# Two units' maxima transposed side by side in one PSUM bank, and stand-in products in place of a memset of the P @ V bank

## The chip, the cores and the metric

The kernel runs on one NeuronCore of a Trainium2 chip. The metric is the device time of one execution in microseconds (us). The profile is that of one execution, taken by the hardware profiler. The engines are TensorE (PE; its weight loads are listed as PEld), VectorE (DVE), ScalarE (ACT), GpSimd (POOL) and SyncE (SP), which here only issues transfers.

## The reference, cut to what matters

Two attentions over the same x (2048 tokens, 512 channels, 32 heads of 16) are mixed by a gate. Side A is plain attention over all 2048 keys. Side B is attention within segments of 512 tokens, masked, plus a memory term that is linear in the queries.

```python
p = softmax(q_A @ k_A.T * 0.25);  a = (p @ v_A) @ wo_A
for s in range(4):                       # segments of 512 tokens
    p = softmax(q_B[s] @ k_B[s].T * 0.25 + mask)
    o[s] = g * (phi(q_B[s]) @ M) / (phi(q_B[s]) @ z + 1e-6) + (1 - g) * (p @ v_B[s])
    M, z = M + phi(k_B[s]).T @ v_B[s], z + sum(phi(k_B[s]))
out = gate * a + (1 - gate) * (o @ wo_B)
```

A softmax subtracts the maximum of each row of scores ahead of its exponential. The change is about how that maximum gets to where it is subtracted.

## The kernel before, in words

**Two stages.** Up to about 326 us the kernel projects x to q, k and v for both sides, stores them to HBM, and begins with the maxima. Then comes the long loop over score slots, and from about 1810 us the last output products.

**Units and slots.** A unit is a side, a group of four heads and a chunk of 512 queries; there are 32 of side A and 32 of side B, mostly taken in turn A, B, A, B (line 99). An A unit has 64 slots and a B unit 10 (`SLOTS`), together 2368, so that a pair of units takes 74 slots. In a slot (`score_part`, line 641) PE multiplies keys by queries into one of three `st` banks (line 656) and ACT takes the exponential into SBUF (line 679). The products use half of PE's rows each: four heads stand as h = 0, 1 in rows 0 to 49 and h = 2, 3 in rows 64 to 113, and slots take the heads in the order 0, 2, 1, 3.

**Maxima, 96 slots ahead.** In the same slot PE makes a second product, of queries by keys, for a unit that is 96 slots (`LEAD`) further on (`max_part`, line 207; products at line 204), into one of four `sm` banks, and DVE reduces it to row maxima (lines 219, 240, 244). For the masked blocks of side B, ACT copies the bank to SBUF (line 230), POOL masks the copy, and DVE reduces it eight slots later (line 234).

**From maxima to scores.** When a unit's last maximum is made, `finish_max` (line 176) has DVE reduce the partial maxima (line 180 or 182) and POOL split the negated result into a rounded part and its remainder, `ms` (lines 187, 188). The unit goes on the list `late` with a due slot: the slot m of its last maximum + 18 (line 248). `transpose_max` (line 191) then takes an `st` bank, transposes `ms` with an identity product (line 194, 32 columns of weights, 128 columns streamed, fp32, which the profile shows as two passes), has ACT copy the bank's 32 rows to `mt` (line 196), and has SP issue two transfers from `mt` into rows 48, 49 and 112, 113 of the unit's q tile (line 198). The k tiles hold ones in those rows, so that the product of a score has the maximum subtracted already. A unit's first score waits for the first of its two transfers (rows 48, 49: heads 0 and 1), its second score, of head 2, for the other.

**Bursts.** After every third slot (`BURST`) comes what is not a score: products P @ V of probabilities that are at least three (A) or five (B) slots old, three pieces a time or four when the queue is long (`some_values`, line 691; line 712), or pieces of the output product (line 789, four strips of 32 columns); then the transposes that are due (line 887). P @ V gathers all pieces of a unit in one bank, `ops` (line 608); each of the four heads has a strip of 32 rows, of which 17 are written, and ACT copies the whole bank out when a unit is done (line 716). For that the bank is set to zero once, by DVE (line 609). After the bursts of slots 2 and 5, when there is no P @ V yet, PE makes three products of the identity by itself into the bank's first 128 columns (line 885).

**Order.** The order of all engines is written out: each engine works through its instructions in the order of these calls. SP's list holds, beside the transfers of the maxima, loads of k (lines 158, 159), q (146, 147) and v (623, 626), and the stores.

Of the kernel before, what the change touches and what calls it, by code (L numbers as in the profile page):

```python
# [10 lines left out]
F32 = mybir.dt.float32  # L11
F32R = mybir.dt.float32r
# [28 lines left out]
MASK_T = 8  # L41
LATE_T = 8
# [5 lines left out]
def gated_mix(ctx, tc, x, xT, wqkv, a_wo, b_wq, b_wk, b_wv, b_wo, beta, gate_w, out):  # L48
    nc = tc.nc
# [24 lines left out]
    identf = const.tile([128, 128], F32, name="identf")  # L74
# [18 lines left out]
    mp = ctx.enter_context(tc.tile_pool(name="mp", bufs=2))  # L93
# [18 lines left out]
    for k in range(NU):  # L112
        mine = {u: iter(range(32)) for u in range(2)}
        bs = [k - 1] if 0 < k < NU - 1 else [k - 1, k] if k else []
        start, apart = (34, 3) if k == 1 else (6, 7) if k < NU - 1 else (24, 3)
        theirs = {r: [(unit("B", b), (r, i)) for b in bs for i in range(5)] for r in range(2)}
        for p in range(64 + 10 * len(bs)):
            r = (len(maxs) + 1) % 2
            i = (p - start) // apart
# [8 lines left out]
    qt, kt_ = {}, {}  # L128

    def raw(t):  # L130

        return t[:].bitcast(F32)
# [36 lines left out]
    late = []  # L169
# [6 lines left out]
    def finish_max(u):  # L176
        nm = mp.tile([128, 4, 4], F32, tag="nm", name="nm")
        pm = pmt.pop(u)
        if u[0] == "A":
            nc.vector.tensor_reduce(nm, pm, axis=AX.X, op=ALU.max, negate=True)  # L180
        else:
            nc.vector.tensor_reduce(nm.rearrange("p h (a b) -> p (h a) b", b=2),
                                    pm.rearrange("p b h (a k) -> p (h a) b k", a=2), axis=AX.X, op=ALU.max, negate=True)

        ms = mp.tile([128, 2, 2, 2, 4], F32R, tag="ms", name="ms")
        nv = nm.rearrange("p (r h) s -> p r h s", r=2)
        nc.gpsimd.tensor_copy(ms[:, :, 0], nv)  # L187
        nc.gpsimd.tensor_sub(ms[:, :, 1], nv, ms[:, :, 0].bitcast(F32))
        return ms

    def transpose_max(u, ms, pool, tag):

        pt = pool.tile([128, CH], F32, tag=tag, name="mt_ps")
        nc.tensor.matmul(pt[:32, :128], ms.rearrange("p r a h s -> p (r a h s)").bitcast(F32), identf, start=True, stop=True)  # L194
        mt = mp.tile([32, 128], F32R, tag="mt", name="mt")
        nc.scalar.copy(mt, pt[:32, :128])  # L196
        for r in range(2):
            nc.sync.dma_start(raw(qt[u])[64 * r + 48:64 * r + 50], raw(mt)[16 * r:16 * r + 16])

    def blocked(ps):  # L200
        return ps.rearrange("p (b t) -> p b t", t=128)

    def max_product(ps, u, h, s, n0, n, k, k0=0):
        nc.tensor.matmul(ps[:, n0:n0 + n], rows(qt[u][:, :, s * 128:(s + 1) * 128], h, 48), rows(k[:, :, k0:k0 + n], h, 48),  # L204
                         start=True, stop=True)

    def max_part(m, bank):

        u, (r, i) = maxs[m]
        side, g, c = u  # L210
        if u not in pmt:
            pmt[u] = mp.tile([128, 4, 4, 4], F32, tag="pmA", name="pm") if side == "A" else pmB[(c * NG + g) % 2]
        pm = pmt[u]
        ps = bank()
        if side == "A":

            kc, s, h = i // 8, i % 8 // 2, 2 * r + i % 2
            max_product(ps, u, h, s, 0, CH, kt_[u, kc])
            nc.vector.tensor_reduce(pm[:, h, s, kc:kc + 1], ps, axis=AX.X, op=ALU.max)  # L219
        else:  # L220


            k = kt_[u, c]
            h0 = 2 * r
            if i < 2:
                for n in range(4):
                    b = i + 2 * (n % 2)
                    max_product(ps, u, h0 + n // 2, b, 128 * n, 128, k, 128 * b)
                dg = dp.tile([128, 4, 128], F32, tag="dg", name="dg")
                nc.scalar.copy(dg, blocked(ps))  # L230
                nc.gpsimd.affine_select(out=dg, in_=dg, pattern=[[0, 4], [-1, 128]], base=0, channel_multiplier=1,  # L231
                                        compare_op=ALU.is_ge, fill=MASKED)
                to = pm[:, i, h0:h0 + 2, 3::4] if i == 0 else pm[:, i, h0:h0 + 2, 1::6]
                todo.append((m + MASK_T, lambda: nc.vector.tensor_reduce(  # L234
                    to, dg.rearrange("p (h s) t -> p h s t", h=2), axis=AX.X, op=ALU.max)))
            elif i < 4:
                h = h0 + i - 2
                max_product(ps, u, h, 1, 0, 128, k)
                max_product(ps, u, h, 3, 128, 384, k)
                nc.vector.tensor_reduce(pm[:, 1, h, 3:7], blocked(ps), axis=AX.X, op=ALU.max)  # L240
            else:
                for f in range(2):
                    max_product(ps, u, h0 + f, 2, 256 * f, 256, k)
                nc.vector.tensor_reduce(pm[:, 0, h0:h0 + 2, 4:6], ps.rearrange("p (h b t) -> p h b t", h=2, b=2), axis=AX.X,
                                        op=ALU.max)
        if m == last_max[u]:
            def finish():
                late.append((m + MASK_T + 2 + LATE_T, u, finish_max(u)))
            todo.append((m + (MASK_T + 1 if side == "B" else 0), finish))

    def run_todo(m):

        for e in [e for e in todo if e[0] <= m]:
            todo.remove(e)
            e[1]()

    def run_late(pool, tag, m):
        for e in [e for e in late if e[0] < m]:
            late.remove(e)
            transpose_max(e[1], e[2], pool, tag)  # L260

    loaded = [0]

    def loads(m):

        m = min(m, len(maxs) - 1)
        while loaded[0] <= m:
            u, (r, i) = maxs[loaded[0]]
            if loaded[0] == first_max[u]:
                load_q(u)  # L270
            kc = u[2] if u[0] == "B" else i // 8
            if (u, kc) not in kt_:
                load_k(u, kc)
            loaded[0] += 1
# [3 lines left out]
    with ExitStack() as p0:  # L278
# [264 lines left out]
        def some_max():  # L543
            m = mnext[0]
            if m == LEAD:
                return
            loads(m + 3 + PRE)
            for i in range(4):
                max_part(m + i, lambda: me_sm.tile([128, CH], F32, tag="sm", name="sm"))
            run_todo(m + 3)  # L550
            mnext[0] += 4
            run_late(me_ps, "me", mnext[0])
# [53 lines left out]
    banks = [sm_ps.tile([128, CH], F32, name=f"sm{i}") for i in range(4)]  # L606

    ops = o_ps.tile([128, CH], F32, name="ops")
    nc.vector.memset(ops, 0.0)

    wos = {}

# [239 lines left out]
    def jam(n):  # L852


        if n < first["A", 0, 1]:
            return len(queue) > 10
        return (len(queue) > 6) + (len(queue) > 13 and n >= first["A", 0, last])
# [3 lines left out]
    while n < nS or queue or beside or filled[0] < len(fill):  # L861
        for f in beside.pop(n, []):
            f()
        if n < nS:
            score_part(n)
        m = n + LEAD
        if m < nS:
            loads(m + PRE)

            def bank():  # L870
                i = free.pop(0)
                free.append(i)
                return banks[i]
            max_part(m, bank)
        run_todo(m)
        if n % BURST == BURST - 1 or n >= nS:
            if shared:
                for _ in range(4):
                    shared.pop(0)()
            else:  # L880
                some_values(n, MOST + jam(n) if n < nS else 8)
            if n < 6:

                for _ in range(3):
                    nc.tensor.matmul(ops[:, :128], identf, identf, start=True, stop=True)

            if any(e[0] < m + 1 for e in late):
                run_late(st_ps, "st", m + 1)
            else:
                if filled[0] < len(fill) and fill[filled[0]][0] <= n:  # L890
                    fill[filled[0]][1]()
                    filled[0] += 1
        n += 1
# [11 lines left out]
def build():  # L905
    import concourse.bacc as bacc
    nc = bacc.Bacc("TRN2", target_bir_lowering=False, num_devices=1)
    shapes = {"x": (S, D), "xT": (D, S), "wqkv": (D, 3 * D), "a_wo": (D, D), "b_wq": (D, D), "b_wk": (D, D),
              "b_wv": (D, D), "b_wo": (D, D), "beta": (H,), "gate_w": (D,)}
    args = [nc.dram_tensor(n, s, F32, kind="ExternalInput").ap() for n, s in shapes.items()]  # L910
    out = nc.dram_tensor("out", (S, D), F32, kind="ExternalOutput").ap()
    with tile.TileContext(nc) as tc:
        gated_mix(tc, *args, out)
    return nc
# [23 lines left out]
```

## Time and profile before

| | |
|---|---|
| time, median of 3 runs | 1890.31 us (1885.98 to 1891.0) |
| time of the profiled execution | 1884.44 us |
| its span, first to last instruction | 1882.4 us |
| busy: PE, DVE, ACT, POOL | 99%, 85%, 80%, 17% |
| granted clock of TensorE | 1.0 |
| transposes of maxima (line 194) | 64, as 128 passes of 273 ns (median) |
| ACT's copies of them (line 196) | 64, 254 ns (median) |
| transfers of the maxima (line 198) | 128, issued in 617 (A) and 660 ns (B) (medians) |
| memset of the P @ V bank (line 609) | 1, 485 ns |

A row of the trace names a line, an engine, an operation and tiles as "out<-in". [...] Transfers appear as issues on SP (SPq); the time of landing is that of the last update of the transfer's semaphore.

### The profile page before, as it was taken

To read this page: it belongs to the slowest core of one execution; us is meant where nothing else is said; L and a number is where in the kernel's file an instruction comes from. 1 tells how busy PE (TensorE), PEld (TensorE's weight loads), DVE (VectorE), ACT (ScalarE), POOL (GpSimd) and SP (SyncE) were. 2 spreads that over 40 slices of the span, in tenths; PEclk is the share of its full clock that TensorE was granted. 3 is DMA by queue.
4 is the path that set the end of the run, shared out by engine and by line. 5 is a ranking of instruction groups with operands and counts; after the bars stand their busy time and mean duration, and the time that the engine had idled before them with its cause. 6 is when DMAs were issued, how large, how long until landed. Compare 5 with 4: busy or idle time off the path is not lost.

```text
span 1882.4 us, 46526 instructions
## 1 busy us (share of the span) xinstructions
PE 1865.2 (99%) x18149; PEld 1008.7 (54%) x18149; DVE 1596.0 (85%) x2746; ACT 1508.0 (80%) x2929; POOL 314.9 (17%) x515
## 2 busy tenths in 40 slices
PE   9999999999999999999999999999999999999999
PEld 7887676555555554444444444444444455555546
DVE  4235777999999999999999999999999999999820
ACT  5445444898988898888888888888888888888884
POOL 3001222111111111111111111212121211111210
PEclk9999999999999999999999999999999999999999
DMA  7567555234343434343434343434343434333311
GB/s 243 193 227 253 196 183 194 83 112 136 88 109 87 113 91 112 94 115 99 114 95 113 102 113 102 113 98 113 98 111 102 113 103 115 102 103 101 89 55 48
DMA packets 124170, 227.31 MB, mean 121 GB/s; under 512 B 34952, under 2 KB 49960, under 8 KB 123440
## 3 DMA queue, kind: packets, MB, share of 16 engines
q1 hardware_dynamic: 122448, 222.68, 41.1%
q8 instruction: 144, 2.36, 0.6%
q0 software_dynamic: 1216, 1.14, 0.2%
q14 instruction: 74, 0.61, 0.1%
q10 hardware_dynamic: 288, 0.52, 0.1%
HBM read 155.52 MB, written 67.52 MB: 118 GB/s over the span
## 4 chain that ended last, share of the span: by engine, by line
PE 92%; ACT 3%; DMA 2%; DVE 1%; issue 1%; POOL 1%; SPq 0%; ACTq 0%; POOLq 0%; DVEq 0%
PE ops L712 31%; PE st L656 28%; PE sm L204 14%; PE pr L315 10%; PE ops L789 6%; PE sm L789 1%; ACT p L679 1%; POOL mn L375 1%; DMA raw<-xT 1%; PE mt_ps L194 1%; PE num L497 1%; ACT dg L230 0%; DMA qdA<-q 0%; DMA vs<-wqkv 0%; DMA qdB<-q 0%
## 5 line engine op out<-in xcount | busy, mean ns | idle before, releaser
L679 ACT ACTIVATE p<-st 128x512 f32<-128x512 f32 x2304 | 1222.4, 605 | 173.6 <-PE sm L204 141.5
L219 DVE TENSOR_REDUCE pm<-sm 128x1 f32<-128x512 f32 x2048 | 1282.3, 683 | 64.8 <-PE sm L204 48.7
L204 PE MATMUL sm<-kA,qA 48*128 48x512 f32 x2048 | 739.4, 445 | 0.0
L656 PE MATMUL st<-qA,kA 50*128 50x512 f32 x2048 | 693.7, 436 | 3.7 <-ACT p L679 3.2
L656 PEld LDWEIGHTS st<-qA,kA 50*128 50x128 f32 x2048 | 332.8, 185 | 426.6 <-ACT p L679 364.6
L712 PE MATMUL ops<-p,vA 128*17 128x512 f32 (+3 forms) x5848 | 556.4, 469 | 0.0
L204 PEld LDWEIGHTS sm<-kA,qA 48*128 48x128 f32 x2048 | 332.6, 184 | 20.7 <-DVE pm L219 6.7
L712 PEld LDWEIGHTS ops<-p,vA 128*17 128x17 f32 x5848 | 109.7, 95 | 174.2 <-issue 152.7
L204 PE MATMUL sm<-kB,qB 48*128 48x128 f32 (+2 forms) x896 | 168.6, 291 | 0.0
L204 PEld LDWEIGHTS sm<-kB,qB 48*128 48x128 f32 x896 | 134.4, 186 | 8.8 <-DVE pm L219 2.6
L231 POOL TENSOR_SCALAR_AFFINE_SELECT dg<-dg 128x512 f32<-128x512 f32 x128 | 81.2, 635 | 296.0 <-ACT dg L230 296.0
L187 POOL CAST ms<-nm 128x16 fp32r<-128x16 f32 x64 | 12.6, 196 | 644.9 <-DVE nm L180 399.8
L656 PE MATMUL st<-qB,kB 50*128 50x384 f32 (+3 forms) x512 | 119.8, 342 | 0.6 <-ACT mt L196 0.2
L378 DVE TENSOR_TENSOR q<-full,q 128x512 fp32r<-128x512 f32 x64 | 44.1, 689 | 87.1 <-ACT q L371 86.0
L656 PEld LDWEIGHTS st<-qB,kB 50*128 50x128 f32 x512 | 71.5, 185 | 66.3 <-ACT p L679 54.0
L660 POOL TENSOR_SCALAR_AFFINE_SELECT p<-p 128x512 f32<-128x512 f32 x128 | 78.8, 635 | 90.7 <-ACT p L679 88.5
L240 DVE TENSOR_REDUCE pmB<-sm 128x4 f32<-128x512 f32 x128 | 87.3, 682 | 0.5 <-PE sm L204 0.5
L234 DVE TENSOR_REDUCE pmB<-dg 128x4 f32<-128x512 f32 x128 | 86.7, 678 | 0.0
L712 PE MATMUL ops<-p,vB 128*17 128x128 f32 (+3 forms) x1192 | 86.5, 398 | 0.2
L370 ACT COPY full<-pr 128x512 f32<-128x512 f32 x64 | 37.3, 583 | 50.7 <-PE pr L315 50.4
L230 ACT COPY dg<-sm 128x512 f32<-128x512 f32 x128 | 76.4, 597 | 1.0 <-DVE pmB L234 0.6
L789 PE MATMUL ops<-woA,vA 128*32 128x128 f32 x1664 | 66.9, 278 | 3.3 <-ACT oraw L716 3.3
(146 smaller groups left out, 1558.6 us busy)
## 6 DMA issues: line engine op xcount, KB each, us to landing
kA<-kdA SPq DMA_DIRECT2D x256, 128.0 KB
vA<-vdA SPq DMA_DIRECT2D x31, 544.0 KB
kA<-kdA SPq DMA_DIRECT2D x256, 64.0 KB
qdA<-q SPq DMA_DIRECT2D x32, 256.0 KB
kdA<-q SPq DMA_DIRECT2D x32, 256.0 KB
qdB<-q SPq DMA_DIRECT2D x32, 256.0 KB
qA<-qdA SPq DMA_DIRECT2D x64, 128.0 KB
kdB<-q SPq DMA_DIRECT2D x32, 256.0 KB
```

The costliest lines, as they stand in the source:

```text
L204: nc.tensor.matmul(ps[:, n0:n0 + n], rows(qt[u][:, :, s * 128:(s + 1) * 128], h, 48), rows(k[:, :, k0:k0 + n], h, 48), start=True, stop=True)
L219: nc.vector.tensor_reduce(pm[:, h, s, kc:kc + 1], ps, axis=AX.X, op=ALU.max)
L230: nc.scalar.copy(dg, blocked(ps))
L231: nc.gpsimd.affine_select(out=dg, in_=dg, pattern=[[0, 4], [-1, 128]], base=0, channel_multiplier=1, compare_op=ALU.is_ge, fill=MASKED)
L234: todo.append((m + MASK_T, lambda: nc.vector.tensor_reduce(to, dg.rearrange("p (h s) t -> p h s t", h=2), axis=AX.X, op=ALU.max)))
L240: nc.vector.tensor_reduce(pm[:, 1, h, 3:7], blocked(ps), axis=AX.X, op=ALU.max)
L315: nc.tensor.matmul(ps, l(a, k), r(b, k), start=(n == 0), stop=(n == 11))
L656: nc.tensor.matmul(ps[:, n0:n0 + CH - q0], rows(k[:, :, b * 128:(b + 1) * 128], h, 50), rows(q[:, :, q0:], h, 50), start=True, stop=True)
L660: nc.gpsimd.affine_select(out=x, in_=x, pattern=[[0, 4], [1, 128]], base=0, channel_multiplier=-1, compare_op=ALU.is_ge, fill=0.0)
L679: nc.scalar.activation(p[:, h], ps, AF.Exp, scale=SCALE)
L712: nc.tensor.matmul(ops[32 * h:32 * h + 17, q0:q0 + 128 * w], v[:, 17 * h:17 * h + 17], p[:, h, c0:c0 + 128 * w], start=(i == 0), stop=done ...
L789: nc.tensor.matmul(ps[32 * t:32 * t + 32, 128 * (j % (ps.shape[1] // 128)):128 * (j % (ps.shape[1] // 128)) + 128], held[side, c][:, o, 12 ...
```

## The change

Due units are taken from `late` in twos. Both are transposed into one bank: the first into partitions 0 to 31, the second into 32 to 63, by products in the first and the second strip of 32 columns of PE (`tile_position`). One copy by ACT takes both, and SP issues the four transfers, those of the first unit first. An A unit is due four slots earlier than before, 14 slots after its last maximum. The memset of the bank of P @ V is dropped; the products of the identity after slots 2 and 5 are now four each, one for every 128 columns, so that they write the whole bank.

```diff
-    def transpose_max(u, ms, pool, tag):
+    def transpose_max(us, pool, tag):
+        w = 32 * len(us)
         pt = pool.tile([128, CH], F32, tag=tag, name="mt_ps")
-        nc.tensor.matmul(pt[:32, :128], ms.rearrange("p r a h s -> p (r a h s)").bitcast(F32), identf, start=True, stop=True)
-        mt = mp.tile([32, 128], F32R, tag="mt", name="mt")
-        nc.scalar.copy(mt, pt[:32, :128])
-        for r in range(2):
-            nc.sync.dma_start(raw(qt[u])[64 * r + 48:64 * r + 50], raw(mt)[16 * r:16 * r + 16])
+        for i, (_, u, ms) in enumerate(us):
+            nc.tensor.matmul(pt[32 * i:32 * i + 32, :128], ms.rearrange("p r a h s -> p (r a h s)").bitcast(F32), identf,
+                             start=True, stop=True, tile_position=(0, 32 * i))
+        mt = mp.tile([64, 128], F32R, tag="mt", name="mt")
+        nc.scalar.copy(mt[:w], pt[:w, :128])
+        for i, (_, u, ms) in enumerate(us):
+            for r in range(2):
+                nc.sync.dma_start(raw(qt[u])[64 * r + 48:64 * r + 50], raw(mt)[32 * i + 16 * r:32 * i + 16 * r + 16])
...
-                late.append((m + MASK_T + 2 + LATE_T, u, finish_max(u)))
+                late.append((m + MASK_T + 2 + LATE_T - (4 if side == "A" else 0), u, finish_max(u)))
...
     def run_late(pool, tag, m):
-        for e in [e for e in late if e[0] < m]:
-            late.remove(e)
-            transpose_max(e[1], e[2], pool, tag)
+        while us := [e for e in late if e[0] < m][:2]:
+            for e in us:
+                late.remove(e)
+            transpose_max(us, pool, tag)
...
     ops = o_ps.tile([128, CH], F32, name="ops")
-    nc.vector.memset(ops, 0.0)
...
             if n < 6:
-                for _ in range(3):
-                    nc.tensor.matmul(ops[:, :128], identf, identf, start=True, stop=True)
+                for i in range(4):
+                    nc.tensor.matmul(ops[:, 128 * i:128 * i + 128], identf, identf, start=True, stop=True)
```

## The prediction

> **What bounds the kernel now.** I read the stages of the span first, then the groups that touch a transpose, then single bursts on DVE, PE and SP in order of time. In the page, and in the stages cut from the steady loop, the columns are us, busy time and instructions by engine:
>
> ```profile
> PE 1865.2 (99%) x18149; PEld 1008.7 (54%) x18149; DVE 1596.0 (85%) x2746; ACT 1508.0 (80%) x2929; POOL 314.9 (17%) x515
> ```
>
> ```profile
> 400.00:700.00 300.00, 299.58 (x3054) 152.72 (x3042) 292.49 (x501) 267.34 (x529) 45.68 (x86) 1.00 0.36 98
> 700.00:1100.00 400.00, 397.98 (x3965) 186.60 (x3957) 385.68 (x662) 351.90 (x695) 68.19 (x116) 1.00 0.40 105
> 1100.00:1500.00 400.00, 397.30 (x3966) 184.66 (x3964) 386.09 (x663) 351.12 (x691) 68.42 (x115) 1.00 0.41 109
> ```
>
> PE is always "busy", but its matmuls overlap. DVE's reduces do not hide so much: 97% of each stage, 96.4% from 700 us on. Where nothing but scores, maxima and P @ V is in a burst (400 such bursts, 1.88 us each), DVE idles 0.036 us of it: there DVE is the bound and PE waits for its banks. All of DVE's idle time from 411 to 1750 us is 48 us, and it gathers where PE comes late, as after a transpose. So a saving on PE ends the run earlier only as far as DVE was waiting for PE at that place.
>
> **The transposes.** This is the group that the change halves:
>
> ```profile
> L194 PE MATMUL mt_ps<-identf,ms x128: 272/273/297, 309.8 to 1811.8; 128*32 128x128 f32 x128
> L196 ACT CAST mt<-mt_ps x64: 246/254/262, 310.2 to 1812.1; 32x128 fp32r<-32x128 f32 x64
> ```
>
> Which ones pair follows from the due slots. From unit A2 on, a B unit's last maximum comes 4 slots before that of the next A unit. B is due 18 slots after its own, A now 14: the same slot, so both are found after the same burst, and it is B's old burst. That holds for 29 pairs; A0, B0, A1 and the last three stay single. 64 copies become 35, and 29 bursts of an A transpose lose it.
>
> What such a burst costs is seen around a B and an A transpose, PE first, then DVE (start, duration, idle before):
>
> ```profile
> 1075.40 1.05 PE L712 MATMUL ops<-p,vA 128*17 128x512 f32 x8
> 1076.27 0.38 PE L194 MATMUL mt_ps<-identf,ms 128*32 128x128 f32 x2
> 1076.58 0.50 PE L656 MATMUL st<-qA,kA 50*128 50x512 f32 x1
> 1078.41 0.50 PE L656 MATMUL st<-qA,kA 50*128 50x512 f32 x1
> ```
>
> ```profile
> 1075.07 1.89 DVE L219 TENSOR_REDUCE pm<-sm 128x1 f32<-128x512 f32 x3 [0.30 <-PE sm L204]
> 1077.15 1.29 DVE L219 TENSOR_REDUCE pm<-sm 128x1 f32<-128x512 f32 x2 [0.19 <-PE sm L204]
> 1078.98 0.69 DVE L219 TENSOR_REDUCE pm<-sm 128x1 f32<-128x512 f32 x1 [0.55 <-PE sm L204]
> ```
>
> The two passes start 0.109 us apart and the scores follow, so that a transpose holds the stream of PE for 2 x 0.109 = 0.218 us. Does the second of a pair cost it again? The nearest row is the output product, with the same shape (32 columns, 128 streamed, fp32) in four strips:
>
> ```profile
> 1089.38 0.64 PE L789 MATMUL ops<-woA,vA 128*32 128x128 f32 x16
> ```
>
> 16 passes start within 0.46 us (the next 16 at 1089.84); in the single records four strips start 7 ns apart, and the next four passes 0.109 us later. So a pair costs 0.218 + 0.007 us, and 29 x 0.218 = 6.3 us of PE go. If strips did not overlap, nothing would go.
>
> How much of it ends the run? For each of the 29 A transposes I took DVE's idle time in the 2 us behind it. It depends on how many slots lie between the pair's burst and B's first score: with 7, 0.17 us up to 600 us of the span and 0.36 later; with 8, 0.33 and 0.20; with 9, next to none. Summing the smaller of 0.218 and the idle time gives 2.0 + 1.8 + 0.2 = **4.0 us**. The bounds are 0 (DVE finds another wait) and 6.3 (what PE gains beyond is kept as a lead). I take 4.0: in plain bursts DVE leaves no room for a lead. ACT's 29 copies (29 x 0.254 = 7.4 us) I cost at nothing: DVE's idle time was ended by PE's products, and ACT idles 0.26 us in a plain burst. Were they not hidden, it would be a gain: rival 1.
>
> **A rule on the array.** The first pass of a transpose starts 0.109 us after the last pass of P @ V in its strip, the same distance as between passes of one kind; and the scores start 0.10 us after the last pass has streamed, with a transpose or without. So nothing but two passes goes with a transpose. [...]
>
> **The transfers.** Four are now issued in a row, A's first; B's score is the one that is near.
>
> ```profile
> 979.67 1.31 SPq L198 DMA_DIRECT2D qB<-mt  x2
> 981.08 0.34 SPq L158 DMA_DIRECT2D kA<-kdA  x1
> 982.91 1.28 SPq L198 DMA_DIRECT2D qA<-mt  x2
> ```
>
> Two issues on SP take 1.31 us; issues of a unit are 0.67 us apart, and the semaphore's last update comes 1.93 us after an issue (medians). So B's transfers land 2 x 0.67 = 1.34 us later than before. SP is free at B's place; the loads of k behind move back by 1.3 us and are asked for 20 slots (13 us) ahead. Before, counted from B's transpose, with 0.13 us from landing to product (as the last B unit shows, whose score starts 0.13 us behind its landing): with 7 slots the two transfers land at 3.34 and 3.99 us and the scores that need them start at 5.21 and 5.56. After: landings at 4.68 and 5.33, scores due 0.218 earlier, at 4.99 and 5.34, so the second is held 0.12 us (early in the run, where ACT's copy ends 0.4 sooner but the scores 0.8, 0.50). With 8 slots: landings 4.00 and 4.67, scores due 4.35 and 4.58, held 0.22 (early 0.38). With 9, the second score lies behind another burst: not held. In all 7 x 0.12 + 3 x 0.50 + 7 x 0.22 + 2 x 0.38 = 4.6 us in which PE is held at B's second score. What hides it: DVE still has a reduce or two of 0.60 us in hand there (at 1078.98 above it starts three in a row, one of a masked copy), and the next scores wait for ACT's exponential anyway. Only in the three early pairs with 7 slots does the next burst find DVE without work: 3 x 0.2 = **+0.6 us**. Bounds: 0 and 4.6.
>
> A's maxima: POOL ends A's `ms` 4 us or more before B's transpose, so that the earlier place adds no wait.
>
> **The start of the loop.** DVE, then PE:
>
> ```profile
> 328.99 0.48 DVE L609 MEMSET ops<- 128x512 f32 x1
> 330.96 1.29 DVE L219 TENSOR_REDUCE pm<-sm 128x1 f32<-128x512 f32 x2 [0.36 <-PE sm L204]
> ```
>
> ```profile
> 329.53 0.94 PE L885 MATMUL ops<-identf 128*128 128x128 f32 x6 [1.12 <-DVE ops L609]
> 331.46 0.94 PE L885 MATMUL ops<-identf 128*128 128x128 f32 x6
> ```
>
> PE waits 1.12 us for the memset, which stands on DVE behind a subtraction. Without it PE goes on at once. Each burst of stand-ins gets two passes more at 0.112 us: 0.22, twice. PE gains 1.12 - 0.45 = 0.67, and DVE, which idles 0.36 and 0.71 us for PE there, gains 0.5 by the memset and is fed sooner: **-0.6 us**. Bounds: -1.1 and +0.45.
>
> **Sum:** -4.0 + 0.6 - 0.6 = -4.0 us. The profiled execution took 1884.44 us (span 1882.4 and 2.0 around it); its like would take 1880.4. It was 5.9 us below the median of the runs shown, 1890.31, which I take as the base: **1886.3 us**, 0.21% less. A measurement of this kernel can hardly tell a change of less than 0.3% (5.7 us) from none: that is within 0.3%.
>
> **Rivals.**
>
> 1. PE counts in full. The score's weight loads wait for ACT 668 times in the steady loop, and the copies taken from ACT may pass on a lead through the `st` banks. Then 6.3 us and the whole 1.1 at the start: 1882.9 us. [...] For it: a burst with a transpose lasts 2.15 us against 1.88. Against: with 9 slots DVE doesn't wait at all. Chance 0.30, of which 0.02 for the drains.
> 2. B's maxima come too late. The mechanism is the one above, at PE's wait ahead of B's scores. If the third and fourth transfer took 2.70 us instead of 1.93, as the slowest of the 128 did, B's scores would be held 7 x 0.89 + 3 x 1.27 + 7 x 0.99 + 2 x 1.15 + 8 x 0.68 + 2 x 0.63 = 26 us in all; cover of 0.38 us a pair (the most that I counted as hidden) takes off 11, and 15 - 4.6 gives 10 us more than before: 1900.7. It decides above (4.6 + 5.7) / 29 = 0.36 us uncovered a pair. For it: the margin is used up already. Against: the slow transfers are all A's, issued just behind loads of k, which B's are not. Chance 0.15.
> 3. It doesn't do what it says: the strips don't overlap, or DVE waits elsewhere, and only the start is gained: 1889.7. The output product's strips speak against it. Chance 0.10.
>
> **Numbers.** Forecast 0.45; with rival 3, within 0.3%: 0.55. Faster 0.30, slower 0.15. The range leaves out the slower rival: from 1881.5 (rival 1 and some drains) to 1893 (nothing gained at the pairs, and more than half of the 4.6 us uncovered).
>
> **What would show it.** Right: 35 copies at line 196; two transposes 7 ns apart; no `mt` on the bursts three to six slots behind; DVE's idle time behind them gone with 7 and 8 slots, unchanged with 9; PE's stand-ins right behind slot 2. Wrong: PE idle ahead of `st<-qB`, ended by the transfers of line 198, with DVE idle behind it; or passes 0.109 us apart in a pair. If DVE idles as long per pair as before, the step from PE's time to DVE's has failed.

## The result and the profile after

| | before | after |
|---|---|---|
| median (range), 7 runs each | 1891.00 us (1885.98 to 1893.84) | 1882.97 us (1881.15 to 1885.85) |
| profiled execution | 1884.44 us | 1883.44 us |
| its span | 1882.4 us | 1881.7 us |
| granted clock in it | 1.0 | 1.0 |

The ratio after to before is 0.9958, with a 95% interval of 0.9944 to 0.9971: 8.0 us, faster by 0.42%. The time lies in the range that was given, but "within 0.3%" was forecast. Two things need explaining: 8.0 us are more than the 4.0 us that were worked out, and the two profiled executions lie only 1.0 us apart. Among the experiments below, two executions took far longer at full clock (4085.99 us of before, 5843.68 us of the start alone); they are left out of ratios and counts.

The page of after, and the same three stages of the steady loop as before (length, then busy time of PE, PEld, DVE, ACT and POOL, clock, DMA share and GB/s):

```profile
PE 1863.1 (99%) x18153; PEld 1006.1 (53%) x18153; DVE 1596.5 (85%) x2745; ACT 1502.9 (80%) x2900; POOL 314.9 (17%) x515
```

```profile
400.00:700.00 300.00, 298.37 (x3040) 151.69 (x3042) 292.64 (x500) 266.42 (x522) 46.00 (x86) 1.00 0.36 98
700.00:1100.00 400.00, 397.75 (x3966) 186.01 (x3968) 386.84 (x663) 350.87 (x687) 68.36 (x116) 1.00 0.41 106
1100.00:1500.00 400.00, 397.02 (x3971) 183.75 (x3963) 386.88 (x664) 350.21 (x685) 69.32 (x118) 1.00 0.41 108
```

DVE is the engine to watch: it does the same work, so more of it in a stage means a faster stage. From 700 us on it is busy 0.8 to 1.2 us more in each 400 us; from 400 to 700 us it gains 0.15 us only.

**The transposes** of after, by tile (minimum, median and maximum in ns, first and last start in us, shapes):

```profile
L196 PE MATMUL mt_ps<-identf,ms x128: 269/273/297, 305.0 to 1807.2; 128*32 128x128 f32 x128
L199 ACT CAST mt<-mt_ps x35: 246/267/280, 305.4 to 1807.9; 64x128 fp32r<-64x128 f32 x29, 32x128 fp32r<-32x128 f32 x6
```

29 copies take two units and 6 take one. A pair late in the run whose first score of B comes 8 slots later, PE and then DVE:

```profile
1073.11 0.39 PE L196 MATMUL mt_ps<-identf,ms 128*32 128x128 f32 x4
1073.43 0.50 PE L660 MATMUL st<-qA,kA 50*128 50x512 f32 x1
```

```profile
1074.00 3.17 DVE L223 TENSOR_REDUCE pm<-sm 128x1 f32<-128x512 f32 x5 [0.31 <-PE sm L208]
1077.70 0.69 DVE L223 TENSOR_REDUCE pm<-sm 128x1 f32<-128x512 f32 x1 [0.54 <-PE sm L208]
```

Four passes take 0.39 us where two took 0.38, and in the single records the second strip starts 5 to 8 ns behind the first. DVE idles 0.31 us behind the pair, as it did behind B's transpose alone; the 0.19 us that it idled behind A's is gone.

**The start of the loop**, PE and then DVE:

```profile
327.74 0.63 PE L208 MATMUL sm<-kB,qB 48*128 48x128 f32 x4
328.30 1.16 PE L890 MATMUL ops<-identf 128*128 128x128 f32 x8
```

```profile
328.77 2.48 DVE L223 TENSOR_REDUCE pm<-sm 128x1 f32<-128x512 f32 x4
332.42 0.69 DVE L223 TENSOR_REDUCE pm<-sm 128x1 f32<-128x512 f32 x1 [1.17 <-PE sm L208]
```

The stand-ins follow slot 2 with no wait. By slot 12 after is 0.54 us earlier than before.

**The transfers** of a pair early in the run, with 7 slots to B's first score, SP (whose entries are the issuing of transfers) and then PE:

```profile
411.87 1.30 SPq L202 DMA_DIRECT2D qA<-mt  x2
413.22 1.27 SPq L202 DMA_DIRECT2D qB<-mt  x2
```

```profile
410.89 0.39 PE L196 MATMUL mt_ps<-identf,ms 128*32 128x128 f32 x4
415.24 0.47 PE L660 MATMUL st<-qB,kB 50*128 50x512 f32 x1
415.90 0.47 PE L660 MATMUL st<-qB,kB 50*128 50x512 f32 x1 [0.16 <-ACT p L683]
```

B's second score starts 5.01 us behind the transpose. The page puts part of that wait down to the transfers, which before did not stand there as a releaser (the last columns are the idle time before the group, and what ended most of it). First the row of before, then that of after:

```profile
L656 PE MATMUL st<-qB,kB 50*128 50x384 f32 (+3 forms) x512 | 119.8, 342 | 0.6 <-ACT mt L196 0.2
L660 PE MATMUL st<-qB,kB 50*128 50x384 f32 (+3 forms) x512 | 120.4, 341 | 2.6 <-DMA qB<-mt 1.2
```

**The end.** The last slot ends 2.15 us earlier than in the profile of before, but the span is only 0.69 us shorter. In the chain that ended last, after shows the transfers of the last output products in place of PE's own closing products (18.42 us of them in the chain of before):

```profile
1858.68 4.01 DMA odA<-oraw
...
1862.71 3.02 DMA rec<-odA
...
1866.36 3.14 DMA rdA<-rec
...
1869.56 3.60 DMA inv<-rdA
```

Nothing of the change touches these. How much the end varies is seen in a second profile of the unchanged kernel (the first experiment): 0.64 us behind the first one at the last slot, 1.42 us at the end. So 1 us between two profiles says little here, and the parts are read slot by slot.

### The profile page after: what moved, and what is told of

Read it like the earlier page. It is cut to its first block, busy times and chain, and to the rows that moved or that the text cites. A ratio compares the mean times of both kernels' runs of the same rounds, so it can differ in the third digit from the quotient of the medians.

```text
span 1881.7 us, 46459 instructions
## 1 busy us (share of the span) xinstructions
PE 1863.1 (99%) x18153; PEld 1006.1 (53%) x18153; DVE 1596.5 (85%) x2745; ACT 1502.9 (80%) x2900; POOL 314.9 (17%) x515
## 3 DMA queue, kind: packets, MB, share of 16 engines
q0 software_dynamic: 1216, 1.14, 0.2%
## 4 chain that ended last, share of the span: by engine, by line
PE 90%; ACT 4%; DMA 3%; DVE 1%; issue 1%; SPq 1%; POOL 1%; ACTq 0%; POOLq 0%; DVEq 0%
PE ops L716 30%; PE st L660 27%; PE sm L208 14%; PE pr L320 11%; PE ops L793 6%; ACT p L683 2%; ACT dg L234 1%; DMA qB<-mt 1%; PE num L502 1%; POOL mn L380 1%; SPq L202 0%; DMA qdB<-q 0%; PE sm L793 0%; PE mps L533 0%; DMA raw<-wqkv 0%
## 5 line engine op out<-in xcount | busy, mean ns | idle before, releaser
L767 DVE RECIPROCAL rec<-rec 128x32 f32<-128x32 f32 x44 | 15.1, 344 | 66.0 <-DMA rec<-odA 35.3
```

## The theories

Beside the time, each execution has a mean granted clock of TensorE. In the runs below, before stands either at 0.999 to 1.000 or between 0.992 and 0.997, after at 0.999 or 1.000. **The theory**: the 8.0 us have three sources. In most executions of before, the 1.12 us that PE waits for the memset make the clock fall to half for a while; the change takes the wait away, and with it the half clock. Then there is the gain at the start at full clock, and at the pairs the worked-out gain of DVE, of which part is lost because A's transfers go first. **The rivals**: the longer executions of before have nothing to do with the memset (spread); it is the two passes more of each stand-in burst, not the wait, that keeps the clock up; at the pairs, the missing share is lost elsewhere than at the transfers; and what the pairs bring comes from ACT's copies saved, not from the strips on PE.

The kernels were run in three groups, each with executions of before beside it. A kernel is compared with those of its own group.

## Experiments: the start of the loop

**Before, unchanged.**

> The kernel before, unchanged, once more. The two profiles at hand differ by 0.7 us of span (1882.4 and 1881.7), while the medians differ by 8.0 us (1891.0 and 1883.0). Spread theory: the profile of before (1884.4) was a short execution of a kernel that mostly takes about 1891; a new profile then shows some 1889 to 1893 and where the 5 to 7 us lie; its runs lie between 1885 and 1894 again. Rival: the kernel's profiled execution is always short and the difference comes with the timed runs alone; the new profile then shows 1882 to 1885 once more. Either way the ratio to before is 1.000 within 0.002, which is the noise of the method.

Median 1893.64 us, ratio 1.0019 (1.0003 to 1.0034). Its profiled execution took 1885.87 us at clock 1.000; the other eleven took 1891.2 to 1898.0 us at 0.992 to 0.996. So its profile is again of the rare kind, and shows nothing of the difference, while its times do: one kernel, two groups of times, told apart by the clock.

**The pairs alone**: after, with the memset and the three stand-ins of before.

```diff
     ops = o_ps.tile([128, CH], F32, name="ops")
+    nc.vector.memset(ops, 0.0)
...
-                for i in range(4):
-                    nc.tensor.matmul(ops[:, 128 * i:128 * i + 128], identf, identf, start=True, stop=True)
+                for _ in range(3):
+                    nc.tensor.matmul(ops[:, :128], identf, identf, start=True, stop=True)
```

> Only the pairs: maxima transposed two by two with A due at 14 slots, but the memset by DVE and the three stand-ins as before. Pair theory (the prediction's mechanism, PE's passes removed): 0.9965 to 0.9975, nearly all of the 0.9958 of the whole change. Start theory (the memset's wait on PE is what costs most executions several us): 0.9985 to 1.000, since the two profiles differ by only 1.6 us over the pairs.

Median 1888.70 us, ratio 0.9995 (0.998 to 1.001): no faster than before. 9 of 12 executions had a lower clock; the other three took 1882.77, 1882.97 and 1884.81 us. The three lie 3.7 us below the executions of before at full clock (1886.64, the median of 12 in the same group), and the nine at the lower clock 2.9 us below those of before at a lower clock (1890.05 against 1892.99). So the pairs bring something on either clock; the median hides it, because here 9 of 12 executions are at the lower clock and in before 16 of 28. The profile of this kernel caught the half clock. First the page's slices (the eighth, from 331 to 378 us, is at 7 tenths), then PE at the start, and three stretches whose ends are taken from the trace's record of the clock:

```profile
PEclk9999999799999999999999999999999999999999
```

```profile
330.35 1.01 PE L891 MATMUL ops<-identf 128*128 128x128 f32 x6 [1.13 <-DVE ops L614]
331.29 0.79 PE L661 MATMUL st<-qA,kA 50*128 50x512 f32 x1
```

```profile
327.66:331.07 3.41, 2.27 (x16) 1.69 (x15) 1.96 (x4) 3.15 (x6) 0.08 (x1) 1.00 0.66 241
331.07:358.38 27.31, 27.31 (x169) 15.55 (x172) 16.80 (x28) 14.96 (x29) 2.48 (x4) 0.50 0.29 82
358.38:385.69 27.31, 27.08 (x279) 13.12 (x277) 26.02 (x45) 24.55 (x50) 3.97 (x9) 1.00 0.17 52
```

The score that lasts 0.49 us elsewhere lasts 0.79 here. For 27.3 us the granted clock is 0.50, although PE is busy without a break; 169 products get through, where the next 27.3 us take 279. This execution took 1893.94 us, 11.0 more than the middle one of the three at full clock.

**The start alone**: before without its memset, with the four stand-ins of after (the last two hunks of the change).

> Only the start: no memset, four stand-ins that fill the bank, transposes one by one as before. Pair theory: 0.9997 (the 0.54 us that the profile after shows by slot 12). Start theory: 0.996 to 0.997, and a narrower spread of its runs than that of before.

Median 1884.95 us, ratio 0.9976 (0.9964 to 0.9988); none of 11 executions below 0.999. The start alone gives 4.7 us, the pairs alone nothing that the median shows. That rules out spread as the cause of the lower clock, and the theory that little is gained at the start.

**Wait and passes apart.** Before with its memset and four stand-ins instead of three:

```diff
-                for _ in range(3):
-                    nc.tensor.matmul(ops[:, :128], identf, identf, start=True, stop=True)
+                for i in range(4):
+                    nc.tensor.matmul(ops[:, 128 * i:128 * i + 128], identf, identf, start=True, stop=True)
```

> The kernel before with four stand-ins over the whole bank after slots 2 and 5, the memset kept: the wait of 1.1 us stays, the passes are those of the change. Wait theory (a 3.41 us window of the clock's record that holds the whole 1.1 us of PE's idle time is followed by half clock for up to 27 us): half clock in about two thirds of the runs, as before, ratio 0.999 to 1.001. Passes theory (more stand-ins keep the clock): full clock in all runs, ratio 0.9975 to 0.998.

Median 1889.06 us, ratio 0.9991 (0.9971 to 1.0011); 6 of 12 at the lower clock. And before without the memset, with as many passes as before in all:

```diff
-    nc.vector.memset(ops, 0.0)
...
-                for _ in range(3):
-                    nc.tensor.matmul(ops[:, :128], identf, identf, start=True, stop=True)
+                for i in range(4 if n < 3 else 2):
+                    nc.tensor.matmul(ops[:, 128 * i:128 * i + 128], identf, identf, start=True, stop=True)
```

> The kernel before without the memset, with four stand-ins after slot 2 and two after slot 5: six in all, as many as before, and no wait. Wait theory: full clock in all runs, 1884.5 to 1885 us, ratio 0.9975 like the start alone. Passes theory: half clock in about two thirds of the runs, ratio 0.9995.

Median 1885.88 us, ratio 0.9969 (0.9957 to 0.9981); 0 of 12. So it is the wait for the memset, and not the number of passes.

**A shorter wait**: a memset of a quarter of the bank, the rest written by the three stand-ins.

```diff
-    nc.vector.memset(ops, 0.0)
+    nc.vector.memset(ops[:, 384:], 0.0)
...
-                for _ in range(3):
-                    nc.tensor.matmul(ops[:, :128], identf, identf, start=True, stop=True)
+                for i in range(3):
+                    nc.tensor.matmul(ops[:, 128 * i:128 * i + 128], identf, identf, start=True, stop=True)
```

> The kernel before with a memset of the last 128 columns only and three stand-ins on the first three blocks of 128: the memset is shorter, so that PE's wait should fall from 1.13 to about 0.8 us. Wait theory with a bound: in a profile at full clock one window held 0.92 us of the wait, in one at half clock it held 1.13, so the bound lies between; at 0.8 all runs keep the full clock, ratio 0.9975 to 0.998. Wait theory without a bound (each us of idle time has its chance): half clock in about half of the runs, ratio 0.999.

The memset took 165 ns, and PE waited 0.72 us:

```profile
328.64 0.94 PE L885 MATMUL ops<-identf 128*128 128x128 f32 x6 [0.72 <-DVE ops L609]
```

Median 1886.21 us, ratio 0.9978 (0.9962 to 0.9994); 1 of 12 at the lower clock. With a wait of 0.72 us it happened once in 12.

In all: with the wait of 1.12 us, 81 of 112 executions had a mean clock under 0.9985 (before in the three groups 16 of 28, 26 of 31 and 13 of 17; before unchanged, the pairs alone and the kernel with wait and four stand-ins 11, 9 and 6 of 12). Without it, 1 of 62. A single window at half clock is too short for this count: the profiled execution of the kernel with wait and four stand-ins has one, shown below, and a mean of 0.999. Eight executions stand at 0.999, three with the wait and five without it; which of the others had such a window is not known.

**Why not always?** In the record of the clock the changes in the loop come in steps of 3.413 us: the stretches of half clock last 1 and 8 such steps, the stretches of full clock behind them 455 and 449. In the profiles of before and of after the one stretch of full clock, 1877.33 and 1873.92 us, is 550 and 549 of them. So I read the record as one of windows of 3.413 us, which begin at another place of the program in each profile (in the four below one starts at 327.66, 326.73, 325.67 and 325.59 us); their ends are counted from the changes of the clock. Four profiles have the wait of 1.12 us. In two of them it lies in one window whole, and the next windows are at half clock: the pairs alone (first of the three lines above: 2.27 us busy of 3.41), and the kernel with wait and four stand-ins, whose windows are

```profile
326.73:330.14 3.41, 2.27 (x14) 1.30 (x12) 1.28 (x4) 2.62 (x6) 0.00 (x0) 1.00 0.62 223
330.14:333.56 3.42, 3.42 (x16) 3.00 (x17) 1.63 (x3) 1.17 (x4) 0.64 (x1) 0.50 0.67 210
333.56:336.97 3.41, 3.41 (x31) 2.42 (x31) 1.98 (x4) 2.96 (x7) 0.63 (x1) 1.00 0.52 115
```

In the other two, both of before, the wait is split by a window's end, and the clock stays. First the second profile of before, then the one that the prediction was made from:

```profile
325.67:329.08 3.41, 3.19 (x17) 2.06 (x15) 1.11 (x2) 1.90 (x5) 0.03 (x1) 1.00 0.67 237
329.08:332.49 3.41, 2.49 (x20) 2.21 (x21) 2.94 (x6) 2.59 (x7) 0.64 (x1) 1.00 0.60 207
```

```profile
325.59:329.00 3.41, 2.79 (x15) 1.75 (x13) 1.28 (x3) 2.05 (x4) 0.00 (x0) 1.00 0.62 217
329.00:332.41 3.41, 2.88 (x23) 2.48 (x23) 2.89 (x5) 2.58 (x7) 0.64 (x1) 1.00 0.60 194
```

So at this place 0.92 us of idle time in a window (2.49 busy) left the clock alone, and 1.14 us (2.27 busy: the wait and 0.02 us more) did not. If the bound at this place lies between the two, a wait of 1.12 us that falls anywhere is caught in (3.41 - 1.12) / 3.41 = 67% to (3.41 - 1.12 + 2 x 0.20) / 3.41 = 79% of the cases, an estimate from these rows; 72% were seen. That the place of the window decides is argued from four profiles and agrees with the count; no run moved the window.

Idle time alone is not the rule, though. In the profile of the pairs alone a window in the projections holds 1.09 us of idle time, and the next is at full clock. In the last profile of this document (transposes side by side) a window among the closing products holds 1.76 us, as PE waits for DVE, and the next is at full clock too:

```profile
160.41:163.82 3.41, 2.32 (x11) 1.63 (x10) 0.69 (x1) 1.36 (x3) 0.00 (x0) 1.00 1.07 282
163.82:167.24 3.42, 3.42 (x16) 2.81 (x16) 1.94 (x3) 2.46 (x5) 0.00 (x0) 1.00 0.44 107
```

```profile
1873.22:1876.63 3.41, 1.65 (x61) 1.38 (x49) 0.65 (x1) 0.00 (x0) 0.00 (x0) 1.00 0.22 59
1876.63:1880.04 3.41, 3.31 (x122) 3.31 (x125) 1.79 (x4) 0.00 (x0) 0.00 (x0) 1.00 0.19 72
```

Other products stand in these windows than at the start of the loop. What counts beside idle time stays open, and so does why the half clock lasts one window in one profile and eight in the other.

## Experiments: the pairs

**After, once more**, beside the kernels of the second group.

> The changed kernel once more, on the chip of the other three, for the comparison with the start alone and with B first: full clock in all runs, 1882 to 1884 us, ratio 0.9955 to 0.9965. The pairs' own worth is its distance from the kernel with six stand-ins and no wait: 1.6 us by the profiles, 2 us by the runs of the start alone.

Median 1883.38 us (1882.74 to 1884.61), ratio 0.9955 (0.9939 to 0.997); 0 of 9 at the lower clock. Against the start alone with the same passes, 1885.88 us, the pairs are worth 2.5 us; by the profiles, over the 29 pairs, 1.7 here and 1.8 in the first profile of after. Why the times show more than the profiles is open. Worked out were 4.0 - 0.6 = 3.4.

**B first**: after, with a pair's B unit transposed and sent ahead of its A unit.

```diff
-        while us := [e for e in late if e[0] < m][:2]:
+        while us := sorted([e for e in late if e[0] < m][:2], key=lambda e: e[1][0], reverse=True):
```

> The changed kernel with the B unit first in each pair, so that its two transfers are issued ahead of A's. In the profile after, B's second score is held: PE idles 0.07 to 0.19 us ahead of it in 15 of 29 pairs, and B's first 0.02 to 0.21 in four. Prediction's theory (the held time is mostly hidden by DVE): the idle time goes, and the time falls by 0.5 us at most from that of the changed kernel, ratio 0.9955 to 0.996. Rival (late maxima cost what they hold): 2.5 us less, ratio 0.9945.

Median 1880.98 us, ratio 0.9954 (0.9938 to 0.9969), all six executions at full clock: 4.0 us below the start alone of the same group (which has no run of after). It was run once more:

> The changed kernel with B first in each pair, once more, for its distance to the kernel before on another chip and as the base of the next one. From its first profile: 4.3 us less than before over the 29 pairs (0.2 each with 7 and 8 slots, none with 9), 0.5 at the start, full clock in all runs. Expected: 1880.5 to 1882 us, ratio 0.9945 to 0.9955; two and a half us less than the changed kernel's 1883.0 to 1883.4 if late maxima cost what they hold, half a us less if DVE hides them.

Median 1879.95 us (1879.31 to 1881.65), ratio 0.9948 (0.9928 to 0.9967). In it the early pair of above looks like this, SP and then PE:

```profile
413.06 1.32 SPq L202 DMA_DIRECT2D qB<-mt  x2
414.43 1.26 SPq L202 DMA_DIRECT2D qA<-mt  x2
```

```profile
412.08 0.39 PE L196 MATMUL mt_ps<-identf,ms 128*32 128x128 f32 x4
416.29 0.50 PE L660 MATMUL st<-qB,kB 50*128 50x512 f32 x1
416.63 0.92 PE L660 MATMUL st<-qB,kB 50*128 50x512 f32 x2
```

B's second score starts 416.63 - 412.08 = 4.55 us behind the transposes, not 5.01, and the group's idle time falls from 2.6 to 0.9 us:

```profile
L660 PE MATMUL st<-qB,kB 50*128 50x384 f32 (+3 forms) x512 | 119.6, 342 | 0.9 <-DMA qB<-mt 0.4
```

The gain of a pair against before, in us, by the slots from the pair's burst to B's first score, early (up to 700 us) and late in the run, compared slot by slot in the profiles:

| | 7 early (3) | 7 late (7) | 8 early (2) | 8 late (7) | 9 early (2) | 9 late (8) | all 29 |
|---|---|---|---|---|---|---|---|
| after | -0.10 | 0.05 | -0.04 | 0.21 | 0.19 | 0.00 | 1.8 |
| B first | 0.225 | 0.215 | 0.20 | 0.185 | 0.18 | 0.01 | 4.3 |
| worked out for DVE alone | 0.17 | 0.218 | 0.218 | 0.20 | about 0.02 | about 0.02 | 4.0 |

The second profile of B first gives 4.2. So the order of A's and B's transfers alone costs 2.5 us by the profiles; by the times, in different groups, it is 2.0 to 3.4.

**Passes or copies?** B first, with the two transposes in one strip, side by side in columns 0 to 127 and 128 to 255 of the same 32 partitions. One copy takes both, as in after, but the passes do not overlap. Copy and transfers have another shape, and `mt` has one buffer.

```diff
-        w = 32 * len(us)
+        w = 128 * len(us)
...
-            nc.tensor.matmul(pt[32 * i:32 * i + 32, :128], ms.rearrange("p r a h s -> p (r a h s)").bitcast(F32), identf,
-                             start=True, stop=True, tile_position=(0, 32 * i))
-        mt = mp.tile([64, 128], F32R, tag="mt", name="mt")
-        nc.scalar.copy(mt[:w], pt[:w, :128])
+            nc.tensor.matmul(pt[:32, 128 * i:128 * i + 128], ms.rearrange("p r a h s -> p (r a h s)").bitcast(F32), identf,
+                             start=True, stop=True)
+        mt = mp.tile([32, 256], F32R, tag="mt", name="mt", bufs=1)
+        nc.scalar.copy(mt[:, :w], pt[:32, :w])
...
-                nc.sync.dma_start(raw(qt[u])[64 * r + 48:64 * r + 50], raw(mt)[32 * i + 16 * r:32 * i + 16 * r + 16])
+                nc.sync.dma_start(raw(qt[u])[64 * r + 48:64 * r + 50], raw(mt)[16 * r:16 * r + 16, 128 * i:128 * i + 128])
```

> As the kernel with B first, but the two transposes of a pair stand side by side in the columns of the bank (columns 0 to 127 and 128 to 255 of the same 32 partitions), so that both use PE's first strip and their passes can't run at once; still one copy by ACT, over 256 columns, and the same transfers. Stream theory (the gain is PE's two passes): the second transpose takes its 0.218 us in B's burst, and most of the 4.3 us at the pairs go: with 7 slots half to all of it, with 8 slots all (PE is late there in B's burst too), in sum 3 to 5 us more than with strips. Copy theory (the gain is ACT's copy and the st bank saved): the 4.3 us stay within 1 us.

Median 1885.29 us (1883.64 to 1887.17), ratio 0.9971 (0.996 to 0.9982). The copies are as few, at 0.358 us each, and the four passes start 0.109 us apart:

```profile
L199 ACT CAST mt<-mt_ps x35: 246/358/372, 305.3 to 1810.1; 32x256 fp32r<-32x256 f32 x29, 32x128 fp32r<-32x128 f32 x6
```

```profile
1073.03 0.60 PE L196 MATMUL mt_ps<-identf,ms 128*32 128x128 f32 x4
```

Over the 29 pairs it gains 0.0 us against before, where B first gains 4.3. B's second score is not held here: it follows the first as closely as in before (0.34 us with 7 slots, 0.23 with 8 late). So in sum the gain goes with the overlap of the strips. ACT saves 29 x (2 x 0.254 - 0.358) = 4.4 us here, and that is worth nothing in sum.

The sum hides two opposite parts, though. With 7 slots this kernel keeps 0.15 us of gain in each of the 10 pairs, without any overlap; with 8 it gains 0.2 early and loses 0.05 late; with 9 late it loses 0.19. So most of the 0.2 us that a pair with 7 slots brings has another source, the one burst in place of two or the copy saved; no run tells these apart. What the overlap brings shows with 8 slots late and with 9.

## Why the prediction was right and wrong

**Where the 8.0 us came from.** The second group has every rung of the ladder on one chip: before 1892.38 us, its five executions at full clock 1887.02 (5.4 less), no wait 1885.88 (1.1 less), and with the pairs 1883.38 (2.5 less): 9.0 us. In the other two groups the half clock makes 3.0 us of before's median (1889.63 against 1886.64 in 12 executions) and 5.8 (1891.57 against 1885.8 in 4). For the 8.0 us of the result that leaves some 4.4 for the half clock, by difference. The start at full clock is 1.1 us here, 1.7 in the first group (1886.64 to 1884.95), 0.5 by the profiles; the split between it and the pairs is good to about 1 us.

- **The step that failed is the base**: "It was 5.9 us below the median of the runs shown, 1890.31, which I take as the base". Those 5.9 us were taken as something that the change leaves alone. Most of them were the half clock behind the memset's wait, which the change removes: 3.0, 5.4 and 5.8 us of before's median in the three groups. The row that carried the wait was in the prediction, priced at 1.12 us and less; the page showed no cost beyond it, because the profiled execution was one of the 28% whose clock stayed up. The term at the start, -0.6, is right at full clock (0.54 by slot 12) and stood for about -5 us in the median.
- **What sets off the half clock is shown only in part.** At the loop's start 1.12 us of idle time in a window that was 66% busy (2.27 of 3.41 us) was enough, a window that was 48% busy (1.65 us) among the closing products did not do it, and in one profile the half clock went on through 27.3 us of unbroken work.
- **DVE's share of a pair's gain held**: 4.0 us worked out, 4.2 and 4.3 measured with B first, and by form too, but for 9 slots early, 0.18 instead of next to none. The agreement with 7 slots does not prove the mechanism: with the transposes side by side 0.15 of that 0.2 us stays, though PE streams all four passes. That the strips overlap held as well (they start 5 to 8 ns apart); that the saved copies bring nothing holds in sum only.
- **How long B's second score is held** also held: with 7 slots early 0.50 us against 0.50 forecast, late 0.14 against 0.12; with 8 slots late 0.27 against 0.22, and only early 0.50 against 0.38. Each is the mean difference to B first, from the transposes to the start of B's second score. In all that is 5.4 us against 4.6.
- **What that costs was mis-sized**: +0.6 us, measured 2.5 by the profiles. The cover was counted in whole reduces. But reduces that last 0.681 us start 0.598 us apart when they follow each other, so that a reduce which starts up to 0.083 us late shows no idle time at all. That is a reason to count less cover; it does not settle the size by form, since with 7 slots late a pair loses 0.17 us for 0.14 held, and with 8 slots late nearly nothing for 0.27.
- **The rivals.** The time of the first, 1882.9 us, was met, but not by its mechanism: PE's savings did not count in full. The range reached down to 1881.5 us for this rival's sake, so that the time lies within it by luck. The drains that its chance and the range also count, time that a transpose would take beyond its passes, are in no run: in before a transpose's first pass starts 0.109, 0.216, 0.322 and 0.429 us (medians; after the same within 0.001) behind the last pass of P @ V in its strip when that has 128, 256, 384 and 512 columns, where passes of P @ V of these widths start 0.120, 0.216, 0.334 and 0.441 us apart; the 0.109 us of the prediction is the first of these. The second's mechanism is real, at 2.5 of the 15 us that it was priced at; that price was for transfers of 2.70 us, and B's took at most 1.98 from issue to landing. The third falls, strips and start both.

Had the two errors been known, the sum would have been 1890.3 - 4.4 - 0.6 - 4.0 + 2.5 = 1883.8 us. The 4.4 are themselves worked out from the result, so this only shows that the parts agree.

## What to carry to other kernels

When a profiled execution lies at the fast end of its own runs, ask what the others have: here the granted clocks of further executions fall into two groups, and a wait of PE of about a microsecond was the place to look. A short wait of PE cost several times its length here (1.12 us cost 3.0 to 5.8 in the median), so a wait for a one-off set-up instruction is worth removing even if the profile at hand prices it at nothing. Where transfers are gathered into one place, issue first the one that is needed first: that alone is worth some 2.5 us here, and B first, at 1879.95 and 1880.98 us, lies below after (1882.97 and 1883.38) and before.

## What the runs showed of the hardware

- TensorE's granted clock fell to 0.50 after a 3.41 us window of the loop's start in which PE was busy for 2.27 us, and stayed after one with 2.49. It also stayed after a window with 2.32 us busy among the projections and one with 1.65 among the closing products. It came back after 3.41 us in one profile and 27.3 us in another, with PE busy throughout.
- Two transposes in two strips of 32 columns hold PE's stream for about 0.22 us (strips 5 to 8 ns apart, the next pass 0.109 us later); in one strip, with the four passes 0.109 us apart, they hold it for 0.44.
- Two executions without the long wait also had a lower clock (one of 12 with the short wait of 0.72 us, at 0.994; one of 12 of the kernel with transposes side by side, at 0.998). Their cause was not looked for.
